# Attention beside a state-space layer on one core: a weight band by two heads, single tail matmuls, another load layout, C swapped by DMA, and a new order of all steps

## The chip, the core and the metric

The kernel runs on one core of one Trainium2 chip. The core has five engines, each with a queue of its own that is worked off strictly in order: TensorE (PE: matmuls and transposes; its weight loads are shown as PEld), VectorE (DVE), ScalarE (ACT), GpSimd (POOL) and SyncE (SP, which here only issues transfers). Transfers run on 16 DMA engines. Matmul results stand in eight PSUM banks and have to be evicted by DVE or ACT. The metric is the device time of one execution in microseconds (us).

## The reference

Two independent layers on inputs of 2048 tokens by 448 features (bf16), their outputs beside each other.

```python
# A: 16 heads of 28; each token attends to 8 tokens, at distances 0, 2, ..., 14
q, k, v = split(x @ wqkv)
idx = pos[:, None] - arange(8) * 2
logits = where(idx >= 0, einsum("bhsd,bhswd->bhsw", q, k[idx]) * 28 ** -0.5, -1e9)
a = einsum("bhsw,bhswd->bhsd", softmax(logits), v[idx]).reshape(B, S, D) @ wo

# B: diagonal complex state space of 448 states
Lam_bar = exp(dt * Lam)
Bu = einsum("bld,pd->blp", x, ((Lam_bar - 1) / Lam)[:, None] * (B_re + 1j * B_im))
h[t] = Lam_bar * h[t - 1] + Bu[t]
b = 2 * einsum("blp,dp->bld", h, C_re + 1j * C_im).real + x * Dskip
out = concatenate([a, b], axis=-1)
```

## The kernel before

**The order.** The kernel has no loops over its work. A string, `ORDER`, lists 580 steps; the last loop of the function calls them one by one, and each step issues one or a few instructions to the queue of an engine. `QK021@24` is step `QK` with arguments 0, 2, 1, and 2 and 4 are the PSUM banks that it takes. A full stop or an equals sign at the end puts an eviction on ACT or DVE. As the queues work in order, `ORDER` alone sets what each engine does next; semaphores hold an instruction until its data have come. The first loads (x, wqkv, B) stand ahead of the string and are issued first. A transfer also waits until the one eight before it is done.

**Part A, attention.** x is loaded in natural layout (`xnA`, row `t * 128 + p` on partition p) and transposed: the first 1024 tokens by PE against an identity (`XI`, `XA`, `XH`, evicted by `xi`, `xa`, `xh`), the others by DMA. The feature dimension of 448 is three blocks of 128 and a tail of 64; two tails, of two token blocks, stand in the two halves of the partitions, so that two 64-row matmuls run beside each other. `QK` and `QS` make q and k (evicted by `qk`, `qh`), `V_` makes v (`v`). For logits, `P` multiplies q on DVE by k shifted by four distances at a time (128x2048 elements, L379), into one of seven buffers, and `E_` sums over each head's features by matmuls against a 0/1 matrix of 32 columns, four of them beside each other in tiles of 128x32 (L391, and L395 for the last heads). `lt` scales the logits to SBUF, `TD` transposes them by DMA (L413), `sma`, `smb` and `smc` are the softmax (maximum and sum on DVE, exponential on ACT).

The weighted sum over v is a matmul against a band matrix, with tokens on both axes. `AL` shifts the weights by matmuls, `al` evicts them to a buffer `Ak` with room between them, `ad` writes that to memory (L497), and `sp` reads it back skewed by one position a row (L503), which gives the band `PT` (128 partitions, 12 blocks, 16 / HS groups, HS * 135 elements). HS = 4 heads are interleaved in a row: neighbouring positions of one head stand four elements apart. `AV` (L528, L534) has v as the stationary operand (32 columns, four heads beside each other) and the band as the moving one, with a step of HS. `W_` (L547) multiplies by wo, `w` evicts to `ya`, `ow` stores.

**Part B, state space.** Tokens are taken in groups of T = 4; the state's 448 complex values are G = 7 groups of 64 real and 64 imaginary ones. `xt` (L696) and `BD` (L672) transpose x and B by DMA to `xTB` and `BT`. `BU` multiplies them (helper `part`, L244, which also serves `QK` and `V_`), `BR` (L723) and `UP` add rotated earlier tokens in the same bank, `z` and `y` evict to `Z` and `Z3`. On DVE `sa` rotates by a table (`ty`, `tf`, `ts` make it), `sb` scans over 256 positions (L764) and `sd` rotates back; `DN`, `dn` and `H_`, `h` carry the scanned state to the other tokens. For the two inner tokens that is done without PE: `sw` swaps real and imaginary halves by DMA, `hp` multiplies by a column (28 steps, all on ACT: L834, L836), `hy` and `hz` add on DVE (L840, L845). C is loaded (`LC`), reordered (`ci`) and transposed by DMA (`CD`) to `Cw`; `ca` multiplies the swapped halves by a column on ACT (two instructions of 64 partitions a group, L684), `cs` multiplies by the other column and adds on DVE (L688). `C` (L859) sums over seven groups, `c` adds x times Dskip (`xd`, L849) on DVE (L867 to L870), `oc` stores. The last tile is done in two halves (`CH`, L884; `ch`, L894; `oh`).

**Order around the change.** PE's queue runs: transposes; q, k and v with the `E_` steps between; from `BU000` on part B with `AL` between; eight `AV`; some `W_` with rotations and corrections; eight `AV`; `W_`, `H_` and the first `C`; and at the end ten `C` and two `CH` steps almost alone. DVE does the 28 `P` steps almost without a break, the first softmax's `sma0` among them, then softmaxes, evictions, scans and corrections, at the end the additions of `c`. SP issues the loads, then `xt0`, `xt1`, `TD0`, `xt2`, `xt3`, `BD`, C's loads and Dskip (`LC`, `LD`), `TD1`, `CD`, wo, and the band's transfers.

Of the kernel before, what the change touches and what calls it, by code (L numbers as in the profile page):

```python
# [15 lines left out]
HALO = 14  # L16
# [4 lines left out]
G = 7  # L21
HS = 4
# [22 lines left out]
z10. BU401@74 BU400 ad0 pm0 smb1 BR11 z11= ts03 smc1 BU010@12 AL1@0 BR21 BU011 al1. BU111@53 xd2 ad1 z40. ca3 cs3 z21.
BU110 BR41 BR12 z12. BR02 z02= BU310@07 BR13 sp0 z13= z41. ts13 BU410@65 xd0 pm1 BR03 z03= sp1 ts04 ca6 ca1 cs6 UP1
BU211@41 BU311 BU411 BR32 z32= BR42 z42= BU210 BR22 ca2 AX@0 BR33 xd1 y1. z33= UP0 y0. BR43 sa0 ax. pm4 cs1 z43= AL2@6
al2. ad2 BU600@32 AL3@0 z22. ts23 al3. ad3 BU601 z60. BU511@64 BR23 z23. cs2 sb0 BU510 sd0 ca4 BR52 z52. UP3 UP4 y4=
UP2 BR61 z61. AV020@0 y3. av020. AV000@3 av000. AV001@6 adx y2= cs4 sa2 sb2 AV011@2 av011= sd2 av001. pm2 AV030@7
AV010@0 AV031@5 AV021@3 av030. BU611@16 ts14 ca5 BU610 BR62 av010. av031. DN0@7 z62. DN1@0 dn1 dn0 sp2 BR53 z53.  # L50
W_20@5 UP5 W_10@1 av021. BR63 W_01@2 W_30@3 y5. ts24 sa4 DN3@4 dn3 DN2@0 sb4 ca0 w20. cs0 z63. ab hp021 hp020 cs5
W_11@7 W_00@5 w01. w11. UP6 spx y6. sp3 AV101@4 av101. AV110@2 w10. w00= AV100@7 AV131@6 AV130@4 av110. AV121@1 sw0
hp120 hp121 AV111@2 AV120@5 av131. dn2 ow11 W_31@0 av111. av100. av120. sd4 DN4@6 sa6 DN5@2 av121. dn4 hp010 ow01 ow20
# [10 lines left out]
def kernel(  # L64
# [45 lines left out]
    def ps(dt=F32):  # L110
        return ps_p.tile([128, 512 if dt == F32 else 1024], dt, tag=f"ps{banks.pop(0)}", name="ps")
# [866 lines left out]
```

## Time and profile before

| | us |
|---|---|
| runs (3) | 128.70, 129.04, 129.21 |
| median | 129.04 |
| profiled execution, first to last instruction (span) | 127.4 |

The page is of one profiled execution, whose time lies within its span and what lies around it: the median of the runs is 1.6 us above the span. PE is busy for 120.3 us of it, DVE 116.0, ACT 104.4, POOL 21.6; PE's clock is granted in full (0.999). The DMA engines move 22.33 MB in 49156 packets.

How to read it: a PE duration contains the pipeline's latency, so that a matmul of 448 columns shows 352 ns while 70 of them pass in 13.36 us (191 ns each); PE's pace is read from starts. In the groups, the columns are line, engine, operation, output<-input, shapes, count, then busy us, mean ns of one, and the idle time ahead of them with what ended it. In stages, each engine has its busy us and a count. In the chain and the time line the columns are start, length, what. SPq is the queue of SP: issues, not the transfers.

### The profile page before, as it was taken

The numbers are of one execution on the slowest core, as the hardware profiler recorded it, in microseconds if no ns is written. First come the engines' busy times: TensorE is split into PE (matmuls) and PEld (weight loads), VectorE is DVE, ScalarE is ACT, GpSimd is POOL, SyncE is SP. The second block draws the span as 40 slices with busy tenths as digits, with TensorE's granted clock in tenths as the row PEclk, the third lists the DMA queues.
The fourth block names the chain that finished last, engine by engine and source line by source line (L and its number), as shares of the span: only waits on it lengthen the run. The fifth ranks groups of instructions, "written<-read, shape, count | busy, mean of one in ns | idle before, by whom it ended". The sixth has DMA issues, their size and how long they took to land.

```text
span 127.4 us, 2887 instructions
## 1 busy us (share of the span) xinstructions
PE 120.3 (94%) x1044; PEld 61.5 (48%) x1053; DVE 116.0 (91%) x223; ACT 104.4 (82%) x205; POOL 21.6 (17%) x41
## 2 busy tenths in 40 slices
PE   6979999999999998999999999999999999999990
PEld 6532443433344442344443558556865545545560
DVE  5679899999998999999899999999999999999651
ACT  0859999997898997899999999999999999961000
POOL 6801000000000000200599992000000000000000
PEclk9999999999999999999999999999999999999999
DMA  3897999899999999487879999993254431234742
GB/s 99 239 223 161 311 263 158 157 231 217 162 246 181 204 217 222 127 165 146 249 320 192 180 339 244 161 132 84 91 145 114 123 109 36 75 110 133 228 144 72
DMA packets 49156, 22.33 MB, mean 175 GB/s; under 512 B 35735, under 2 KB 48599, under 8 KB 49143
## 3 DMA queue, kind: packets, MB, share of 16 engines
q1 hardware_dynamic: 48936, 22.12, 75.7%
q8 instruction: 8, 0.13, 0.4%
q10 hardware_dynamic: 207, 0.04, 0.2%
q14 instruction: 5, 0.04, 0.1%
HBM read 9.86 MB, written 6.37 MB: 127 GB/s over the span
## 4 chain that ended last, share of the span: by engine, by line
PE 82%; DMA 8%; SPq 5%; issue 2%; DVE 0%
PE ps L244 36%; PE ps L859 16%; PE ps L547 10%; PE ps L534 6%; DMA BT<-Bn 5%; PE ps L723 4%; DMA wq<-in_A_wqkv_dram 3%; PE ps L391 2%; SPq L696 2%; SPq L128 2%; PE ps L789 1%; PE ps L348 1%; PE ps L884 1%; PE ps L395 1%; PE ps L461 1%
## 5 line engine op out<-in xcount | busy, mean ns | idle before, releaser
L379 DVE TENSOR_TENSOR pr<-qf,kf 128x2048 bf16<-128x2048 bf16 x24 | 28.2, 1236 | 0.0
L244 PE MATMUL ps<-xbuf,BT 128*128 128x512 bf16 (+1 forms) x107 | 23.5, 380 | 0.9 <-DMA BT<-Bn 0.4
L859 PE MATMUL ps<-Cw,Z 128*128 128x448 bf16 x105 | 20.6, 352 | 0.0
L244 PE MATMUL ps<-xT,wq 128*128 128x512 bf16 (+1 forms) x93 | 19.5, 379 | 0.6 <-issue 0.5
L859 PEld LDWEIGHTS <-Z 128*128 128x128 bf16 x105 | 10.3, 98 | 9.7 <-issue 0.2
L244 PEld LDWEIGHTS <-BT 128*128 128x128 bf16 (+1 forms) x112 | 8.7, 97 | 12.2 <-issue 2.7
L547 PE MATMUL ps<-wo,oT 128*128 128x448 bf16 x64 | 13.9, 353 | 0.0
L244 PEld LDWEIGHTS <-wq 128*128 128x128 bf16 (+1 forms) x96 | 7.7, 97 | 11.2 <-issue 2.3
L114 ACT CAST Z<-ps 128x512 bf16<-128x512 f32 (+1 forms) x24 | 11.7, 522 | 1.3 <-issue 0.9
L935 POOL MEMSET PT<- 128x4320 f32 x3 | 11.0, 3703 | 8.9 <-DVE Z L114 8.9
L244 PE MATMUL ps<-wq,xT 128*128 128x448 bf16 (+1 forms) x64 | 11.7, 353 | 0.0
L684 ACT ACTIVATE ctmp<-Cw,c2t 64x448 f32<-64x448 bf16 x14 | 9.3, 666 | 0.2
L547 PEld LDWEIGHTS <-oT 128*128 128x128 bf16 x64 | 6.2, 98 | 5.5 <-issue 0.2
L534 PE MATMUL ps<-PT,v_s 128*32 128x135 bf16 (+1 forms) x256 | 8.6, 299 | 0.3 <-issue 0.3
L114 ACT CAST ya<-ps 128x448 bf16<-128x448 f32 (+1 forms) x15 | 7.7, 554 | 1.3 <-DMA out_dram<-ya 1.2
L114 ACT CAST oT<-ps 128x512 bf16<-128x512 f32 x15 | 8.3, 613 | 0.1
L244 PEld LDWEIGHTS <-xT 128*128 128x128 bf16 (+1 forms) x64 | 5.2, 97 | 6.0 <-issue 1.5
L114 ACT CAST v_s<-ps 128x448 bf16<-128x448 f32 x16 | 7.8, 545 | 0.1
L114 ACT CAST qf<-ps 128x512 bf16<-128x512 f32 x12 | 6.9, 593 | 1.0 <-PE ps L349 0.7
L534 PEld LDWEIGHTS <-v_s 128*32 128x32 bf16 x256 | 7.1, 111 | 0.8 <-issue 0.5
L723 PE MATMUL ps<-Z,R 128*128 128x512 bf16 x21 | 7.1, 379 | 0.0
L911 POOL MEMSET Z<- 128x14 bf16 x1 | 0.1, 110 | 38.0 <-ACT v_s L114 38.0
(170 smaller groups left out, 221.5 us busy)
## 6 DMA issues: line engine op xcount, KB each, us to landing
PT<-pd SPq DMA_DIRECT2D x16, 156.0 KB, 4.4
out_dram<-ya SPq DMA_DIRECT2D x16, 112.0 KB, 1.8
out_dram<-xbuf SPq DMA_DIRECT2D x15, 112.0 KB, 1.8
pd<-Ak SPq DMA_DIRECT2D x2, 640.0 KB, 3.6
xbuf<-in_A_x_dram SPq DMA_DIRECT2D x2, 448.0 KB
xnB<-in_B_x_dram SPq DMA_DIRECT2D x4, 224.0 KB, 6.3
xnB<-in_B_x_dram SPq DMA_DIRECT2D x4, 192.0 KB, 5.6
PT<-Z SPq DMA_DIRECT2D x6, 128.0 KB, 2.4
```

The source lines that it names most:

```text
L114: (ACT.copy if e == "A" else V.tensor_copy)(o, i)
L128: SP.dma_start(wq[:, 0:3, c + d:c + d + n], wq_r[:, :, c + d:c + d + n])
L244: PE.matmul(o, l, r, start=(first and i == 0), stop=(not first and i == len(pairs) - 1 and not more[s]))
L379: V.tensor_tensor(t[:], q.unsqueeze(1).to_broadcast((128, 4, 512)), k4, ALU.mult)
L391: PE.matmul(acc[s][32 * i:32 * i + 32], E[:, f, ws, :], t[:, i, :], start=(f == 0 and ws == 0), stop=False)
L534: PE.matmul(p[32 * hh:32 * hh + 32, 128 * bl:128 * bl + n], v_s[:, t, 4 * hg + hh, :], PT[:, t % NS, (4 * hg + hh) // HS, (4 * hg + hh) % ...
L547: PE.matmul(p[:, 0:D], late["oT"][:, b // 4, hg, par, 128 * (b % 4):128 * (b % 4) + 128], late["wo"][:, hg, :], start=(hg == 0), stop=(hg ...
L684: ACT.activation(t[a:a + 64, 0:D], Cw[b:b + 64, g, :], ACTF.Copy, scale=c2t[a:a + 64, g:g + 1])
L696: SP.dma_start(xTB[:, :, :, 128 * cb:128 * cb + 128].rearrange("p a b c -> p (a b) c"), xnB[:, cb].rearrange("p j d -> p (j d)"), transpos ...
L723: PE.matmul(pp["z", g, j][:], rot(g, 0), late["Z"][:, g, j - 1, :], start=False, stop=True)
L859: PE.matmul(p[:, 0:D], z, Cw[:, g, :], start=(g == 0), stop=(g == G - 1))
L935: POOL.memset(late["PT"][:, 4 * i:4 * i + 4].rearrange("p t g n -> p (t g n)").bitcast(F32), 0.0)
```

## The change

- `HS` is 2: two heads interleaved in the band. `AV` steps by two elements, `sp` copies twice as many pieces of half the length.
- The tail matmuls of 64 rows are steps of their own (`QT`, `VT`, `BH`); the main ones are by half (`QS`, `VM`, `BU` take one bank and issue three matmuls). `part`, `two`, `QK` and `V_` go.
- x of the first 1024 tokens is loaded with four consecutive rows on a partition (`LX`), one contiguous piece for each partition; the evictions `xi`, `xa`, `xh` write with a step of four to put the tokens in order.
- All loads are steps of the order (`LX`, `LQ`, `LH`, `LV`, `LY`, `LB`, `LN`, `TX`, `WX`).
- C: `CS` writes `Cw` with its halves swapped to a buffer by two transfers, `ca` and `cb` multiply the two by their columns in place (seven each, on ACT or DVE as the order says: of `ca` one on ACT, of `cb` three), `cs` adds two groups at a time on DVE.
- `hp` can go to DVE: 15 of 28 do.
- Buffers that rotated are named by slot in the order (`P`, `ty`, `smc`, `w`, `c`).
- All steps stand in a new order. In SP's queue the loads of C and Dskip stand ahead of the transposes `xt` and `BD`, half of B's load between them, the order of transposes is `xt1`, `xt3`, `xt2`, `BD`, `xt0`, and `TD0` follows. `sma0` stands behind the last `P` on DVE, one `rb` ahead of the first. Evictions of `z` and `y` are on ACT, but for two `y`.

The diff, cut to its core:

```diff
-HS = 4
+HS = 2
...
-    prp = pool("a_pr", bufs=7, c=cl)
+    prp = pool("a_pr", c=cl)
...
+    def LX(a, b):
+        k = a // 4
+        SP.dma_start(xnA[:, a:b], A_x[0, 512 * k:512 * k + 512].rearrange("(p t) d -> p t d", t=4)[:, a - 4 * k:b - 4 * k])
...
     def xi(h, k, e):
-        p, c = pp["xi", h], 256 * h
+        p = pp["xi", h]
...
-            evict(e, xT[:, 0, 0:2, c:c + 256], p[:, 0:512].rearrange("p (f n) -> p f n", f=2))
+            evict(e, xT[:, 0, 0:2].rearrange("p f (n t) -> p f t n", t=4)[:, :, 2 * h:2 * h + 2],
+                  p[:, 0:512].rearrange("p (f t n) -> p f t n", f=2, t=2))
...
-    def QK(u, m, k):
-        p = two("qk", u, m)
-        part(("qk", u, m), k,
...
+    def QS(u, m, s):
+        p = pp["qk", u, m, s] = ps()
         for kt in range(3):
-            PE.matmul(p[:], wqk(m, slice(0, 128), kt), xT[:, 0, 4 * s + kt], start=(kt == 0), stop=False)
-        PE.matmul(p[:], wqk(m, slice(64 * s, 64 * s + 64), 3), xT[64 * s:64 * s + 64, 0, 3], start=False, stop=True)
+            PE.matmul(p[:], wqk(m, slice(0, 128), kt), xT[:, u, 4 * s + kt], start=(kt == 0), stop=False)
+
+    @op
+    def QT(u, m, s):
+        r = slice(64 * s, 64 * s + 64)
+        PE.matmul(pp["qk", u, m, s][:], wqk(m, r, 3), xT[r, u, 3], start=False, stop=True)
...
-    def ca(g):
-
-        t = pp["ctmp", g] = smp.tile([128, 512], F32, tag="z", name="ctmp", bufs=2)
+    def CS():
         for a, b in ((0, 64), (64, 0)):
-            ACT.activation(t[a:a + 64, 0:D], Cw[b:b + 64, g, :], ACTF.Copy, scale=c2t[a:a + 64, g:g + 1])
+            SP.dma_start(late["oT"][a:a + 64, 0].rearrange("p a b n -> p (a b n)")[:, 0:G * D],
+                         Cw[b:b + 64].rearrange("p g n -> p (g n)"))
+
+    def scaled(e, t, c):
+        if e == "A":
+            ACT.activation(t, t, ACTF.Copy, scale=c)
+        else:
+            V.tensor_scalar(t, t, c, None, ALU.mult)
+
+    @op
+    def ca(g, e):
+
+        scaled(e, swc(g), c2t[:, g:g + 1])
+
+    @op
+    def cb(g, e):
+        scaled(e, Cw[:, g, :], c1t[:, g:g + 1])
 
     @op
     def cs(g):
-        V.scalar_tensor_tensor(Cw[:, g, :], Cw[:, g, :], c1t[:, g:g + 1], pp["ctmp", g][:, 0:D], ALU.mult, ALU.add)
-
+        n = 2 if g < 6 else 1
+        o = Cw[:, g:g + n, :].rearrange("p g n -> p (g n)")
+        V.tensor_tensor(o, o, swc(g, n), ALU.add)
...
-    def BU(g, jp, k):
...
+    def BU(g, j):
+        p = pp["z", g, j] = ps()
+        for f in range(3):
+            PE.matmul(p[:], BT[:, g, f, :], xTB[:, j // 2, 4 * (j % 2) + f, :], start=(f == 0), stop=False)
+
+    @op
+    def BH(g, j):
+        r = slice(64 * (j % 2), 64 * (j % 2) + 64)
+        PE.matmul(pp["z", g, j][:], BT[r, g, 3, :], xTB[r, j // 2, 3, :], start=False, stop=(j == 0))
...
-    def hp(k, j, g):
+    def hp(k, j, g, e="A"):
...
-            ACT.activation(t, late["SW"][:, NC * g:NC * (g + 1)], ACTF.Copy, scale=bcol[:, j - 1, g:g + 1])
+            i, c = late["SW"][:, NC * g:NC * (g + 1)], bcol[:, j - 1, g:g + 1]
...
+        if e == "A":
+            ACT.activation(t, i, ACTF.Copy, scale=c)
+        else:
+            V.tensor_scalar(t, i, c, None, ALU.mult)
```

Of the new order, first the loads, then the stretch from the last `E_` steps to the first of part B, and the band's copies:

```
LX02 LX24 LQ00 LQ11 LQ01 LX48 LQ10 LH13 LH01 LV LB110 LH03 LQ21 LH10 LY1 LY2 LH02 LY0 LQ20 LH12 WX LN10 LB001 LD
WU@0 LN00 LB100 XI0@0 TX3 TX0 TX2 TX1 PP@1 LB021 LB111 xi00= LB011 LB120 LC pcopy xi01. pa XI1@2 xi10= LB010 xi11.
XI2@3 LB121 QS000@1 xi20. pb pd_ QS030@3 LB101 QS010@2 QT000 XH1@0 XA10@4 xt1 LB000 pc XA11@5 LB020 LN11 LN01 xt3
xt2 pe ty0@0 ty5@1 BD xt0 QS020@6 tf0 tf5 xa10= pf pg xa11. QS031@4 xh1. ts00 qk000. QS021@5 rb0 QS001@0 VM100@1
QT010 qk010= P000@0 QT001 ts05 ts10 ts20 QT020 QT031 QT030 QT021 qk001. qk021. qk031. qk030. VM000@7 P001@1 qk020.
P021@2 P020@3 VM111@2 VM101@5 QS051@4 ts15 ty2@0 tf2 ts25 QS050@6 QS011@3 QT011 QT050 VT111 ty1@1 qk011. P010@4
...
qk141. qk150. E_06 lt00 qk120. P121@4 QS160@7 QS140@3 qk131. QS121@4 QS161@0 QT160 QT121 lt01 QT140 qk140. QT161
...
VM500@7 VT410 VT511 hc1 VT400 VT011 P131@3 P151@4 P150@5 P130@1 v011. VT500 VT401 v401. v511. ts16 v400. E_13 E_15
P141@2 E_14 ts26 BU21@0 BU00@1 ty3@1 v500. BU30@3 BU11@7 BU10@5 P161@1 P160@2 E_16 BH10 BH11 BH00 v410. sma0 smb0
OZ z10. lt11 lt10 TD1 OP CS tf4 ab dk BH21 BH30 z30. z00. BU12@2 BR11 BU20@5 BU01@4 z11. pm3 BU13@3 smc0@0 BH12 xd0
BH01 pm1 BH20 BH13 BR01 BR12 z12. AL1@7 al1. z01. AL0@1 BU50@2 BU40@7 BU03@4 pm4 al0. ad1 pm0 pm2 sma1 tf3 z20. wo
ad0 rb3 smb1 ts03 smc1@0 ca0= cb2= ca3= cb0= BU31@5 BU41@1 BU02@6 BH02 BH41 BH40 z40. BH03 BH50 BH31 BR13 z13. BR02
...
BR52 z52. BR43 z43. DN0@6 dn0 BR61 z61. BU62@7 UP4 y4. BR53 z53. AV001@5 av001. AV010@2 av010. AV031@4 av031.
AV011@6 ad3 sp2 spx AV020@1 AV021@5 AV030@0 AV000@2 sp3 cs4 av011. UP5 BU63@4 BH63 BH62 sd2 DN2@6 BR62 y5. sa4
```

More of the change, by code (lines that the diff above doesn't have):

```diff
@@ L48 @@
[L48 to L52, printed above, removed]
@@ L234 @@
     Cr = s1.tile([128, 4, 2, D], BF16, tag="Cr")
+    prt = prp.tile([128, 7, 4, 512], BF16, tag="pr", name="pr")
+    ltb = prp.tile([128, 2, 512], BF16, tag="lt", name="lt")
     pp = {}
     ops = {}
[L238 to L251 removed]
     def op(f):
@@ L912, in OZ @@
         late["sc"] = s5
-        late["m"] = 0
     @op
@@ L924, in OP @@
                       late["ya"].rearrange("p k n -> p (k n)")[:, 0:2560]]
-        late["n"] = 0
     @op
```

204 lines of the change are left out of this document (91 added, 113 removed).

## Prediction

> **What bounds the kernel now.** I read the page's head first, then the busy time by stage, then the chain that ended last, then single stretches of the time line.
>
> ```profile
> span 127.4 us, 2887 instructions
> PE 120.3 (94%) x1044; PEld 61.5 (48%) x1053; DVE 116.0 (91%) x223; ACT 104.4 (82%) x205; POOL 21.6 (17%) x41
> ```
>
> Three engines are nearly full, so the mean shares decide nothing. The stages do (columns: length of the stage, then busy time of PE, PEld, DVE, ACT, POOL with counts, clock, DMA share, GB/s):
>
> ```profile
> 3.60:9.53 5.93, 5.06 (x43) 2.89 (x44) 4.32 (x20) 3.96 (x14) 2.46 (x9) 1.00 0.96 224
> 9.53:49.24 39.71, 38.56 (x276) 15.69 (x281) 38.61 (x60) 37.26 (x78) 0.61 (x1) 1.00 1.04 207
> 49.24:114.10 64.86, 64.10 (x645) 35.08 (x651) 63.05 (x125) 61.48 (x114) 16.05 (x11) 1.00 0.66 160
> 114.10:124.60 10.50, 10.03 (x60) 5.54 (x57) 7.86 (x20) 0.97 (x2) 0.00 (x0) 1.00 0.52 168
> ```
>
> Up to 49.24 us PE, DVE and the DMA engines are all full (DMA share 1.04). From there to 114.10 PE and DVE are both full: PE idles 0.76 us, DVE 1.81. So a gain on one of them alone gives nothing; the later of the two sets the end. Only the last 10.5 us belong to PE alone. The chain and DVE's time line show the three points at which they meet:
>
> ```profile
> 24.43 1.41 PE ps L391 x24
> ...
> 42.46 6.74 DMA BT<-Bn
> ...
> 109.43 13.36 PE ps L859 x70
> 122.79 1.35 PE ps L884 x14
> ...
> 124.17 0.39 DVE xbuf L894
> ```
>
> ```profile
> 48.27 2.36 DVE L379 TENSOR_TENSOR pr<-qh_t,kh 128x2048 bf16<-128x2048 bf16 x2
> ...
> 113.41 0.69 DVE L845 TENSOR_TENSOR Z<-Z,PT 128x1024 bf16<-128x1024 bf16 x1
> ```
>
> ```profile
> 49.24 2.22 PE L244 MATMUL ps<-xbuf,BT 128*128 128x512 bf16 x11 [0.43 <-DMA BT<-Bn]
> ```
>
> First point: the state part's first matmul (BU) starts at 49.24, when the transposed weights BT land. Second: DVE ends its last product for the logits (P) at 50.63. Third: DVE ends the last scan correction (hz) at 114.10, and PE needs it in the C step that it has just begun; from there PE runs to 124.14 without a gap, 10.04 us. An output addition of 0.39 and the last store follow, to 127.4.
>
> **The change, part by part.**
>
> *Weight band by two heads.* The matmuls that apply the attention weights (AV) read every fourth element of the band, in the change every second. Their rate now:
>
> ```profile
> 76.89 4.11 PE L534 MATMUL ps<-PT,v_s 128*32 128x135 bf16 x128
> 80.93 0.39 PE L244 MATMUL ps<-xbuf,BT 64*128 64x512 bf16 x2
> ```
>
> From 76.89 to 80.93 128 matmuls pass, four beside each other: 32 sets in 4.04 us, 126 ns for a set of some 133 columns, 0.95 ns a column. The logits' matmuls (L391, the same 128x32 tiles, operand contiguous) pass six sets of 512 columns in 1.41 us, a change of tile shape included: 0.46 ns a column. So AV runs at half the rate, and its step is the difference that I see. If a step of two gives the full rate, a set takes some 60 ns: 64 sets by 66 ns, 4.2 us off PE. If it doesn't, 0. No row has a step of two. I take 4.2: steps of one and four give 0.46 and 0.95, so if the time goes with the bytes spanned, a step of two gives 0.95 / 2 = 0.48, about the contiguous rate. [...]
>
> The band's copy out of memory (sp) gets pieces of 156 bytes for 312, with the same bytes.
>
> ```profile
> PT<-pd SPq DMA_DIRECT2D x16, 156.0 KB, 4.4
> ```
>
> ```profile
> 80.80 2.13 SPq L503 DMA_DIRECT2D PT<-pd  x4
> ```
>
> ```profile
> 88.54 0.66 PE L534 MATMUL ps<-PT,v_s 128*32 128x135 bf16 x16
> ```
>
> If a piece costs the same whatever its size, landing goes from 4.4 to 8.8 us. The cover is the work between the first eight AV steps and the second eight: sp3 overwrites what the first eight read, in both versions. That stretch takes 7.5 us of PE before (81.0 to 88.5); by the new order it has eight W steps and some rotations, of about the same length. The four issues (2.13) and 4.4 leave 1 us of margin, so the cost is 0 to 3.4 us; I take 0, as the bytes don't grow.
>
> *Matmul tails as own steps.* The number of matmuls of every shape stays. By the two orders PE changes tile shape 45 times for 48. At some 0.1 us (1.41 less six sets at 0.22) that is 0.3 us off PE.
>
> *Swapped C by DMA, and scalings moved.* I counted DVE's instructions from its last P to its last hz, 122 before and 132 after, and priced them by these rows:
>
> ```profile
> L834 ACT ACTIVATE PT<-PT,bcol 128x512 bf16<-128x512 bf16 x8 | 5.8, 745 | 0.0
> L684 ACT ACTIVATE ctmp<-Cw,c2t 64x448 f32<-64x448 bf16 x14 | 9.3, 666 | 0.2
> L688 DVE SCALAR_TENSOR_TENSOR Cw<-Cw,c1t,ctmp 128x448 bf16<-128x448 bf16 x7 | 4.6, 675 | 0.0
> L114 DVE CAST Z<-ps 128x512 bf16<-128x512 f32 x5 | 3.4, 687 | 0.2 <-PE ps L723 0.2
> L114 DVE CAST Z<-ps 128x256 bf16<-128x256 f32 x6 | 2.4, 418 | 0.0
> L114 DVE CAST oT<-ps 128x512 bf16<-128x512 f32 x2 | 1.3, 674 | 0.0
> L114 DVE CAST ya<-ps 128x448 bf16<-128x448 f32 x2 | 1.2, 617 | 0.0
> L666 DVE TENSOR_TENSOR R<-Is,co 128x896 bf16<-128x896 bf16 x2 | 2.2, 1084 | 0.0
> L849 DVE TENSOR_TENSOR xnB<-xnB,dsk 128x1792 bf16<-128x1792 bf16 x4 | 4.3, 1083 | 0.0
> L869 DVE TENSOR_TENSOR xbuf<-ps,xnB 128x384 bf16<-128x384 f32 x8 | 4.4, 549 | 0.2 <-PE ps L859 0.2
> L867 DVE TENSOR_TENSOR xbuf<-ps,xnB 128x448 bf16<-128x448 f32 x7 | 4.1, 618 | 2.0 <-PE ps L859 2.0
> L845 DVE TENSOR_TENSOR Z<-Z,PT 128x1024 bf16<-128x1024 bf16 x4 | 2.6, 686 | 0.0
> L757 DVE TENSOR_TENSOR vv<-Z,tab 128x512 bf16<-128x512 bf16 x3 | 1.3, 426 | 0.1
> L649 DVE TENSOR_SCALAR kM<-iot,fT 128x256 f32<-128x256 f32 x7 | 2.4, 346 | 0.0
> L705 DVE COPY dsk<-dsk 128x384 bf16<-128x384 bf16 x1 | 0.3, 254 | 0.0
> ```
>
> ```profile
> 40.41:42.70 2.29, 1.96 (x7) 1.00 1.13 209
> ```
>
> Out of this stretch go: seven L688 (4.73), five wide and four narrow Z evictions to ACT (3.44 and 1.67), one oT and one ya eviction (1.29), one R (1.08, now before the first P), one Dskip product (1.08, now after), two L869 less one L867 (0.48): 13.8 us. In come: the first softmax's maximum (five instructions; the window row has them and the ends of two neighbours, 1.96), four sums of C (448 or two times 448 columns, 0.4 and 0.6 by L757 and L845: 2.2), and 25 multiplications by a column, ten of C and 15 of the correction. The last kind isn't in the trace on bf16. Its floor is the copy L705, 254 at 384 columns (270 to 290 here); its ceiling L757, 426. I take 340, as L649 is the same operation: 8.5 us, 7 to 10.5. In all 12.7 come in: DVE's stretch gets shorter by 1.1, and as much of the shown durations overlaps with the next instruction (two products of L379 in 2.36 us) and ten more instructions overlap more, I take 1.8 (bounds 0 and 3.5). ACT loses 14 L684 and 15 products at 745, 20 us, and takes some 8 back (the evictions as priced above, four scalings of C at 0.65): it is off the path, and its earlier evictions let DVE and PE wait less. Of DVE's 1.81 us of idle time I take 0.8 as gone (0 to 1.8).
>
> C's swap is two transfers more, 0.8 MB, while the DMA share is 0.66; DVE reads them late, behind both softmax ends, so 0.
>
> *First loads and all steps reordered.* Before the first P DVE gets one R (1.08) more and the first softmax's maximum (1.9) less; three evictions of x, 2048 columns, now write every fourth element, 0 to 1.0 us (twice the 0.5 ns a column between L757 and L845). The last P stays at 50.6, by 0.5 either way. PE's 0.87 us of idle time between 3.60 and 9.53 may go, but PE waits for P at E steps before 49, so it gives nothing.
>
> The DMA order changes more. SP now issues C's loads and Dskip before the last transposes, and the first softmax's transpose (TD) behind them:
>
> ```profile
> 37.27 1.26 SPq L413 DMA_TRANSPOSE attn<-lt  x1
> ...
> 47.36 0.57 SPq L268 DMA_DIRECT2D Cr<-in_B_C_re_dram  x1
> ...
> 49.72 0.58 SPq L701 DMA_DIRECT2D dsk<-in_B_Dskip_dram  x1
> ```
>
> ```profile
> 40.00:50.00 10.00, 9.37 (x83) 4.06 (x83) 9.66 (x13) 9.91 (x20) 0.11 (x1) 1.00 1.10 212
> ```
>
> The five issues from 47.36 to 50.30 (2.8 us) go ahead of what the first BU needs, TD's 1.26 goes behind: 1.5 us later by issue. By bytes (0.9 MB at 212 GB/s less TD's 0.26 MB) it is 3.1. Pauses of SP ahead of its transposes, such as this one, may go in the new order:
>
> ```profile
> SPq L413 <- ACT kh L114: 1.1, 1, 1.1
> ```
>
> The contiguous x loads may save some of it too; I don't price that. So BU starts between 48.8 (49.24 less PE's wait of 0.43) and 51.5; I take 50.0, near the middle, and TD's landing, 1.26 more issue and its flight, at 51.5. DVE, done with P at 50.6, then waits 0.9 us for it: a new wait. Behind it in DVE's queue stands all that this engine does to the end.
>
> **The sum.** DVE: 51.5 + 63.5 - 1.8 - 0.8 = 112.4 for the last hz (before 114.10). PE needs that one for the fifth of seven matmuls of a C step, six C steps and 1.35 us follow: 10.2, so 122.6. PE by itself: 50.0 + 74.9 (49.24 to 124.14) - 4.2 - 0.3 = 120.4, earlier, so DVE decides. DVE's own additions behind hz, 24 instructions for 19, take about 10, the same end. 122.6 for 124.14 is 1.5 us less. Against the profiled execution (span 127.4) it gives 125.9; the median of the runs is 129.04, 1.6 above the span, and I take 129.04 - 1.5 = **127.5 us**.
>
> **Rivals.**
>
> *PE at its own floor.* If the multiplications cost their floor and idle time goes, hz ends at 110 and PE's 120.4 decides: 3.7 less, 125.3. For it: ACT is relieved. Against it: DVE's time line has no slack that the change frees for certain.
>
> *AV stays at half rate* (also the case in which the change doesn't do what it says): PE needs 50.0 + 74.9 - 0.3 = 124.6, past DVE: 129.5, from 128.3 (BU at 48.8) to 131. For it: no row shows a step of two. [...]
>
> *Slower: the transposes land late.* Place: SP's queue between C's loads and TD. With the price by bytes and no pause saved, BU starts at 51.5 and TD lands at 53.5 or later; DVE idles 3 us and hz ends at 114.4 or later. From a landing of TD at 53.0 the gain is gone; at 54.5 the time is 130.5. For it: the DMA share is over 1 in this very stage. Against: C's pieces of 896 bytes move faster than a transpose's.
>
> **Chances.** Forecast (126.3 to 128.4) 0.46, PE's floor 0.14, AV unchanged 0.17, late transposes 0.18, others (a late band, friction of banks at the end) 0.05, mostly slower. About 0.5% is what a measurement here can tell from none: 128.4 and 129.7. Faster 0.59, same 0.13, slower 0.28. The range is 125.0 to 130.4: it leaves out the ends of floor and late transposes.
>
> **What would show it.** AV: a set near 60 ns right, near 126 wrong. BU's first matmul near 50 and a DVE wait for the DMA behind the last P. DVE's multiplications near 340 ns. The last hz near 112.4, with PE running from there to the end in about 10.2 us. If PE idles over 2 us behind 50, or AV waits for the band, I am wrong.

## The result, and the profile after

The changed kernel takes 137.1 us (median of 5 runs, 135.07 to 139.39) beside 129.04 before: a ratio of 1.0515 with an interval of 1.0428 to 1.0602. Runs more than 1.5% above the fastest of their kernel are left out of a ratio, so the ratios below, and not the medians, are compared; 1.0515 of 129.04 is 6.6 us slower. The forecast was 127.5. The profiled execution took 135.97 us.

The head of the page after the change:

```profile
span 134.3 us, 2882 instructions
PE 122.4 (91%) x1044; PEld 58.8 (44%) x1053; DVE 121.4 (90%) x235; ACT 93.8 (70%) x190; POOL 22.6 (17%) x41
...
PEclk9999999999999999999999996799999999999998
```

PE is busy 2 us longer although the number of matmuls is the same, DVE 5 us longer, ACT 11 us less, and the granted clock has a dent at 60% of the span. The stages (length, then busy PE, PEld, DVE, ACT, POOL with counts, clock, DMA share, GB/s), cut where PE's long waits at the start are over (16.26), where the state part's first matmul (BU) starts, at the last matmul ahead of a wait (79.03), where the half rate behind that wait ends (85.41), and shortly ahead of the first C step (104.70):

```profile
3.60:16.26 12.66, 9.02 (x47) 4.75 (x49) 8.62 (x27) 8.60 (x19) 2.47 (x9) 1.00 0.97 240
16.26:53.96 37.70, 37.31 (x272) 14.93 (x275) 36.79 (x52) 33.96 (x71) 1.77 (x4) 1.00 1.10 198
53.96:79.03 25.07, 24.77 (x194) 11.01 (x193) 24.27 (x44) 23.76 (x48) 15.96 (x9) 1.00 0.88 199
79.03:85.41 6.38, 3.74 (x11) 1.18 (x9) 5.61 (x15) 2.17 (x5) 0.00 (x0) 0.73 1.27 224
85.41:104.70 19.29, 19.18 (x366) 11.37 (x368) 17.90 (x42) 18.38 (x39) 0.00 (x0) 1.00 0.87 130
104.70:130.96 26.26, 25.80 (x140) 13.28 (x138) 25.64 (x59) 6.18 (x12) 0.00 (x0) 1.00 0.35 111
```

Two stages are new. Up to the point from which PE runs on without long waits, 12.66 us go by with 9.02 of PE, where before it was 5.93 with 5.06; BU, at 49.24 before, now starts at 53.96. And from 79.03 to 85.41 PE is busy for 3.74 of 6.38 us at a mean clock of 0.73. From 85.41 to the end PE has no gap to speak of, as before.

DVE's time line, its start before (first fence), and its start and some later rows after (second; start, length, engine, line, operation):

```profile
4.82 0.62 DVE L114 COPY xT<-ps 128x512 bf16<-128x512 bf16 x2 [0.56 <-PE ps L288]
9.20 0.69 DVE L114 COPY xT<-ps 128x1024 bf16<-128x1024 bf16 x1 [0.48 <-PE ps L305]
9.81 2.76 DVE L379 TENSOR_TENSOR pr<-qf,kf 128x2048 bf16<-128x2048 bf16 x2
```

```profile
4.57 1.30 DVE L125 COPY xT<-ps 128x512 bf16<-128x512 bf16 x1 [0.31 <-PE ps L296]
...
13.78 2.43 DVE L125 COPY xT<-ps 128x1024 bf16<-128x1024 bf16 x1 [2.78 <-PE ps L318]
...
20.44 4.63 DVE L386 TENSOR_TENSOR pr<-qf,kf 128x2048 bf16<-128x2048 bf16 x4
...
53.06 2.36 DVE L386 TENSOR_TENSOR pr<-qh_t,kh 128x2048 bf16<-128x2048 bf16 x2 [0.20 <-PE ps L398]
...
58.04 0.25 DVE L728 COPY dsk<-dsk 128x384 bf16<-128x384 bf16 x1
58.20 0.90 DVE L729 COPY dsk<-dsk 128x64 bf16<-128x64 bf16 x1
...
60.33 0.95 DVE L441 RECIPROCAL zc<-zc 128x128 f32<-128x128 f32 x1
...
65.11 0.86 DVE L654 TENSOR_SCALAR kM<-iot,fT 128x256 f32<-128x256 f32 x1
...
70.98 2.39 DVE L697 TENSOR_SCALAR oT<-oT,c2t 128x448 bf16<-128x448 bf16 x1
73.30 0.32 DVE L697 TENSOR_SCALAR Cw<-Cw,c1t 128x448 bf16<-128x448 bf16 x1
...
118.87 1.89 DVE L873 TENSOR_TENSOR Z<-Z,PT 128x1024 bf16<-128x1024 bf16 x3
```

Three things are to be seen. A copy of 512 columns, two of which took 0.62 us, takes 1.30 now that it writes every fourth element, and one of 1024 columns 2.43 for 0.69. The first product for the logits (P) starts at 20.44 instead of 9.81; the new order has moved some of this by itself (e1 below, without the strided copies, has 14.39), but the last P also ends later, at 55.34 (the instruction behind it starts then) for 50.63. And three instructions in the middle are many times too long: the copy of 64 columns lasts 0.90, longer than the one of 384 ahead of it (0.25); L654 lasts 0.86 for 0.35 elsewhere; a multiplication by a column lasts 2.39 where the next one, of the same shape, lasts 0.32. Beside these three stand GpSimd's memsets:

```profile
58.21 0.86 POOL L957 MEMSET wo<- 128x896 f32 x1 [2.35 <-issue]
59.90 3.71 POOL L959 MEMSET PT<- 128x4320 f32 x1 [0.83 <-DMA Cw<-Cn]
...
64.66 1.17 POOL L955 MEMSET ya<- 128x1280 f32 x1
65.76 7.48 POOL L959 MEMSET PT<- 128x4320 f32 x2
```

The first long one ends as the memset of 58.21 does (59.10, 59.07). The second starts inside the memset of 64.66 and ends near that one's end (65.97, 65.83). The third ends as the pair from 65.76 does (73.37, 73.24). All three are copies or multiplications by a column, with one tensor operand, from SBUF to SBUF; I call these one-operand below. Not everything with one operand is late: the reciprocal at 60.33 takes 0.95 us inside the memset of 59.90, as it does in the kernel before where no memset runs (53.05), and an eviction out of PSUM takes its usual 0.42 there (68.56) beside the memsets of 61.87. PE at the two places, the start and behind the scan:

```profile
8.96 2.29 PE L351 MATMUL ps<-xT,wq 128*128 128x512 bf16 x5 [0.45 <-ACT xT L125]
...
13.80 0.81 PE L351 MATMUL ps<-xT,wq 128*128 128x512 bf16 x3
...
81.94 0.40 PE L800 MATMUL ps<-Z,R 128*128 128x256 bf16 x1 [2.64 <-DVE Z L795]
82.13 1.48 PE L735 MATMUL ps<-xbuf,BT 128*128 128x512 bf16 x3
...
86.93 0.81 PE L735 MATMUL ps<-xbuf,BT 128*128 128x512 bf16 x3
88.00 2.19 PE L539 MATMUL ps<-PT,v_s 128*32 128x135 bf16 x128
```

At 8.96 five matmuls of 512 columns take 2.29 us, the half rate; from 13.80 on three take 0.81. (The clock column gives 1.00 for this stage, so that the half rate is read from the pace. In e5 PE is busy for the same 1.00, 1.00 and 0.64 us of 9 to 10, 10 to 11 and 11 to 12, with as many matmuls, and there the column gives 0.50.) Ahead of 81.94 PE waits 2.64 us for DVE's scan (L795), and then runs at half rate again: three matmuls in 1.48 at 82.13, 0.81 at 86.93. The clock's row for that moment:

```profile
82.00:83.00 1.00, 1.00 (x4) 0.38 (x5) 1.00 (x4) 0.00 (x0) 0.00 (x0) 0.50 1.23 307
```

The last row of PE's time line is the good part: 128 matmuls with the attention weights (AV) in 2.19 us, half of before's 4.11.

### The profile page after: what moved, and what is told of

Same layout as the page of the kernel before. It is cut to its first block, busy times and chain, and to the rows that moved or that the text cites. A ratio compares the mean times of both kernels' runs of the same rounds, so it can differ in the third digit from the quotient of the medians.

```text
span 134.3 us, 2882 instructions
## 1 busy us (share of the span) xinstructions
PE 122.4 (91%) x1044; PEld 58.8 (44%) x1053; DVE 121.4 (90%) x235; ACT 93.8 (70%) x190; POOL 22.6 (17%) x41
## 4 chain that ended last, share of the span: by engine, by line
PE 49%; DVE 17%; ACT 12%; DMA 10%; POOL 3%; issue 3%; SPq 2%; POOLq 1%; DVEq 0%; ACTq 0%
PE ps L351 14%; PE ps L887 12%; PE ps L515 5%; ACT oT L125 4%; DVE xT L125 4%; PE ps L356 3%; DMA PT<-Z 3%; DVE oT L697 3%; DMA out_dram<-ya 3%; POOL PT L959 3%; PE ps L398 2%; PE ps L552 2%; DMA Cw<-Cn 2%; DMA wo<-in_A_wo_dram 2%; ACT Z L125 2%
## 5 line engine op out<-in xcount | busy, mean ns | idle before, releaser
L351 PE MATMUL ps<-xT,wq 128*128 128x512 bf16 x80 | 21.0, 403 | 3.3 <-DVE co L621 1.7
L735 PE MATMUL ps<-xbuf,BT 128*128 128x512 bf16 x80 | 21.7, 397 | 0.2
L125 ACT CAST Z<-ps 128x512 bf16<-128x512 f32 (+1 forms) x33 | 15.6, 527 | 5.9 <-PE ps L747 5.5
L351 PEld LDWEIGHTS <-wq 128*128 128x128 bf16 x84 | 8.2, 102 | 14.8 <-issue 7.1
L735 PEld LDWEIGHTS <-BT 128*128 128x128 bf16 x84 | 8.0, 101 | 9.8 <-issue 2.5
L515 PE MATMUL ps<-wq,xT 128*128 128x448 bf16 x48 | 10.4, 353 | 0.2 <-ACT qh_t L125 0.2
L125 ACT COPY xT<-ps 128x256 bf16<-128x256 bf16 (+2 forms) x5 | 5.2, 1087 | 4.0 <-PE ps L318 2.0
L125 DVE COPY xT<-ps 128x512 bf16<-128x512 bf16 (+1 forms) x3 | 4.9, 1672 | 3.1 <-PE ps L318 2.8
L515 PEld LDWEIGHTS <-xT 128*128 128x128 bf16 x48 | 4.4, 98 | 6.0 <-issue 2.4
L125 ACT CAST kf<-ps 128x512 bf16<-128x512 f32 x11 | 6.1, 597 | 0.7 <-PE ps L356 0.7
```

Source lines behind the costliest of these rows:

```text
L125: (ACT.copy if e == "A" else V.tensor_copy)(o, i)
L351: PE.matmul(p[:], wqk(m, slice(0, 128), kt), xT[:, u, 4 * s + kt], start=(kt == 0), stop=False)
L515: PE.matmul(p[:, 0:D], xT[:, b0 // 4, 4 * s + kt, c + par:c + 256:2], wq[:, kt, 2 * D:3 * D], start=(kt == 0), stop=False)
L735: PE.matmul(p[:], BT[:, g, f, :], xTB[:, j // 2, 4 * (j % 2) + f, :], start=(f == 0), stop=False)
```

## The experiments

After the result I had three theories. **A, the start**: partition-major loads force strided evictions, and these delay the first P and everything behind it. **B, GpSimd's memsets**: in the new order they stand beside one-operand DVE instructions, which wait for them; this makes the scan late. **C, the clock**: it is PE's half rate, at the start and behind the wait at 79, that costs. The prediction's own rival, **late transposes**, and the disputed point **who sets the end**, PE or DVE, were tested with them. Differences in us are ratio differences times 129, and a ± is the intervals of the two runs taken together. The diffs are cut to their core, and of a line of the order only the part that moves is shown. e1 to e6, e9, e10 and e12 start from the changed kernel; e7, e8 and e11 from the kernel before.

**e1_contig.** The first x loads and their evictions as before, all else as changed.

```diff
-        SP.dma_start(xnA[:, a:b], A_x[0, 512 * k:512 * k + 512].rearrange("(p t) d -> p t d", t=4)[:, a - 4 * k:b - 4 * k])
+        SP.dma_start(xnA[:, a:b], xA_r[:, a:b])
...
-        evict(e, o.rearrange("p (n t) -> p t n", t=4), i.rearrange("p (t n) -> p t n", t=4))
+        evict(e, o, i)
...
```

> The changed kernel with its first loads of x and their evictions as before (contiguous), all else kept. Theory A (the early evictions that write every fourth element cost the start): the DVE eviction of 1024 columns falls from 2.43 us to about 0.7, those of 512 from 1.3 to about 0.65, TensorE's waits of 1.37 and 2.03 us behind 5.7 and 14.2 us shrink to under 0.7 each, the first state matmul moves from 53.96 to 50 to 51 us, and the time falls by 3 to 4 us, to about 132. Rival (the order of the first steps holds the start): the evictions get shorter but the first logits product stays behind 18 us, and the time falls by under 1.5 us. Rival (late transposes): the start gets earlier, VectorE then waits over 2 us for the first softmax transpose, and the time falls by under 1.5 us.

Measured: 1.042 (1.0345 to 1.0495), 1.2 ± 1.5 us better than the change, so by its time alone not to be told from none; e6 beside e5 tries the same edit again. DVE's and PE's time lines:

```profile
9.59 0.68 DVE L125 COPY xT<-ps 128x1024 bf16<-128x1024 bf16 x1
...
14.39 4.63 DVE L384 TENSOR_TENSOR pr<-qf,kf 128x2048 bf16<-128x2048 bf16 x4
```

```profile
26.79 4.06 PE L349 MATMUL ps<-xT,wq 128*128 128x512 bf16 x17 [1.76 <-DMA xT<-xbuf]
...
51.22 3.40 PE L733 MATMUL ps<-xbuf,BT 128*128 128x512 bf16 x14 [0.94 <-DMA xbuf<-xnB]
...
79.99 0.28 PE L798 MATMUL ps<-Z,R 128*128 128x256 bf16 x1 [3.29 <-DVE Z L793]
```

The evictions are back at 0.68, the first P at 14.39, the last P's end at 51.67 (3.7 earlier), and BU at 51.22 (2.7 earlier). Theory A holds for the start, but at most a part arrives at the end: PE now waits for transposes by DMA (1.76 and 0.94), which the slow start had hidden, and longer for the scan (3.29 for 2.64).

**e2_chop.** GpSimd's six memsets cut into 30 short ones, to let DVE in between (the expectation counts five and 22).

```diff
...
-            POOL.memset(late["PT"][:, 4 * i:4 * i + 4].rearrange("p t g n -> p (t g n)").bitcast(F32), 0.0)
+            for q in range(8):
+                w = H // HS // 2
+                POOL.memset(late["PT"][:, 4 * i + q // 2, w * (q % 2):w * (q % 2) + w].rearrange("p g n -> p (g n)").bitcast(F32), 0.0)
```

> The changed kernel with GpSimd's five memsets cut into 22 shorter ones, same bytes. Theory B (a copy or a multiplication by a column on VectorE waits for the end of GpSimd's running memset): the three long VectorE instructions, 0.90, 0.86 and 2.39 us, fall to at most 0.7 each (0.2 to 0.35 by themselves plus what is left of a short memset), VectorE gains 2.3 to 3 us, TensorE's wait of 2.9 us at 79.0 falls to under 1 us and its half rate from 82 to 85 us goes; the time falls by 3 to 4.5 us. Rival (the multiplication waits for the DMA that swaps C, or is slow on its first use): the 2.39 us stays and the time falls by under 1 us.

Measured: 1.0841 (1.0772 to 1.091), 4.2 ± 1.4 us worse. DVE, and GpSimd beside it:

```profile
65.35 9.25 DVE L654 TENSOR_SCALAR kM<-iot,fT 128x256 f32<-128x256 f32 x1
```

```profile
66.56 7.89 POOL L963 MEMSET PT<- 128x540 f32 x16
```

One instruction of 0.35 us lasts 9.25, to the end of sixteen memsets in a row (74.45). So the place of theory B is right and the form I gave it is wrong: shorter memsets don't make the wait shorter. Here it lasted to the end of the whole row.

**e3_warm.** Matmuls on a constant tile, overwritten at once, ahead of three early steps and of the scan's rotation, to keep PE's clock up.

```diff
+        for _ in range({(0, 0): 12, (3, 0): 6, (2, 0): 8}.get((m, s), 0) if u == 0 else 0):
+            PE.matmul(p[:, 0:128], wz[:], wz[:], start=True, stop=True)
...
```

> The changed kernel with matmuls on zeros, whose result is overwritten, in TensorE's waits: 26 ahead of the first query and key projections, 46 ahead of the scan's second matmul. Theory C (TensorE runs at half rate behind a wait, and this costs by itself): the pitch of 512 columns falls from 427 to 215 ns between 7 and 12 us and between 82 and 85 us; the time falls by 1.5 to 3.5 us. Rival (the waits cost, the rate only fills time in which TensorE would wait anyway): the pitch falls and the time moves by under 0.7 us.

Measured: 1.0484 (1.0388 to 1.058), 0.4 ± 1.7 us better. The half rate is gone (six matmuls of 512 columns at 9.30 take 1.46 us, and the clock is 1.0 from 79 to 86), the first P comes at 18.43, the last one ends at 53.51 for 55.34, and BU, at 53.04, now waits 0.92 us for the transposes. The time can't be told from the change's; a gain of up to some 2 us isn't excluded. So theory C is shown for the start's delay, and not for the end.

**e4_band4.** The changed kernel with the band by four heads again.

```diff
-HS = 2
+HS = 4
```

> The changed kernel with the weight band by four heads again, all else kept. If TensorE sets the end of the changed kernel, a set of four weight matmuls goes back from about 66 to 126 ns and the time rises by 3.5 to 4.5 us, to about 140. Rival (VectorE sets the end, as the prediction had it): the sets get longer and the time rises by under 1.5 us. Rival (the pieces of 156 bytes cost): the band lands earlier and the time falls.

Measured: 138.95 to 144.28, median 142.4; the runs lie too far apart for an interval. Its profiled execution has two things at once, AV's slower rate on PE and this on DVE:

```profile
64.97 9.33 DVE L654 TENSOR_SCALAR kM<-iot,fT 128x256 f32<-128x256 f32 x1
```

AV is back at 4.07 for 2.19. But L654, untouched by this edit, lasts 9.33 us, to the end of the memsets (74.30, 74.15), where in the change's profiled execution it slipped in after 0.86. So the edit's effect is mixed with the memsets', and e12 was made to part them.

**e5_twoin.** The remedy that follows from e2: the nine one-operand DVE instructions that fall beside the memsets or close to them written in two-operand forms (a product with a column broadcast, a maximum of a tile with itself), in the same places (the expectation calls them eight).

```diff
...
         else:
             V.tensor_scalar(t, t, c, None, ALU.mult)
+        elif e == "T":
+            V.tensor_tensor(t, t, c.to_broadcast((128, D)), ALU.mult)
...
-        V.tensor_copy(dsk[:, 512:896], dsk[:, 0:384])
+        V.tensor_tensor(dsk[:, 512:896], dsk[:, 0:384], dsk[:, 0:384], ALU.max)
```

> The changed kernel with the eight VectorE instructions that stand beside GpSimd's memsets written with two tensor operands (the phase of two frequencies, the two copies of Dskip, five scalings of C), same place, same values. Theory B, sharpened by the last runs (a one-operand copy or multiplication on VectorE waits while GpSimd runs memsets back to back, and is let in only at some joints; the two-operand forms run beside them): no VectorE instruction between 56 and 75 us is longer than 1.3 us, VectorE gains 2.5 us or more, TensorE's wait near 79 us and its half rate behind it shrink, the time is 131 to 133 us and the runs spread by under 1.5 us where they spread by 4. Rival (the long ones wait for data, or the spread comes from the clock): one of them stays above 2 us, or the time stays above 134 us.

Measured: 1.027 (1.0186 to 1.0354), 3.2 ± 1.6 us better than the change.

```profile
65.08 0.48 DVE L657 SCALAR_TENSOR_TENSOR kM<-iot,fT,mag 128x256 f32<-128x256 f32 x1
...
70.58 0.62 DVE L702 TENSOR_TENSOR oT<-oT,c2t 128x448 bf16<-128x448 bf16 x1
```

Nothing waits: the same two steps last 0.48 and 0.62 beside the same memsets. (The form has a price of its own, 0.62 us for the 0.33 that the multiplication takes away from memsets.) PE's wait near 79 falls to 1.67 us and no half rate follows it (the clock is 1.00 from 70 to 90). Theory B is shown: the form of the instruction decides whether DVE waits.

**e6_contig_twoin.** e1 and e5 together (both diffs above).

> The last edit together with contiguous first loads and evictions of x. If the two losses are separate, the gains add: 128.5 to 130.5 us, the kernel before reached again. If the late transposes of the new DMA order take the start's gain back (the first state matmul waits for the transposes at 50 to 51 us, the softmax for its own), it stays at 130.5 to 132 us.

Measured: 1.0139 (1.0076 to 1.0202), 4.9 ± 1.4 us better than the change, about the sum of both (1.2 and 3.2), and 1.7 ± 1.4 better than e5, which is e1's edit again. No version of the new order measured faster, and it is still behind the kernel before. PE and DVE:

```profile
51.92 3.40 PE L740 MATMUL ps<-xbuf,BT 128*128 128x512 bf16 x14 [2.10 <-DMA xbuf<-xnB]
...
78.72 0.28 PE L805 MATMUL ps<-Z,R 128*128 128x256 bf16 x1 [1.64 <-DVE Z L800]
```

```profile
48.85 2.36 DVE L386 TENSOR_TENSOR pr<-qh_t,kh 128x2048 bf16<-128x2048 bf16 x2 [0.19 <-PE ps L398]
53.21 0.29 DVE L422 TENSOR_TENSOR attn<-attn,mk 128x256 bf16<-128x256 bf16 x1 [1.99 <-DMA attn<-lt]
...
114.12 1.90 DVE L878 TENSOR_TENSOR Z<-Z,PT 128x1024 bf16<-128x1024 bf16 x3
```

With both faults mended the prediction's rival is in plain sight: DVE is done with P at 51.2 and waits 1.99 us for the softmax's transpose (TD); PE waits 2.10 for BU's. The last scan correction (hz) ends at 116.0, before 114.10.

**e7_before_band2.** The kernel before with the band by two heads, alone.

```diff
-HS = 4
+HS = 2
```

> The kernel before with the weight band by two heads and nothing else. The sets of four weight matmuls take about 66 ns for 126, 4.2 us less on TensorE. If VectorE and TensorE were both full (the reading of the prediction), VectorE's last correction near 114 us holds the end and the time falls by under 1 us, to 128.2 to 129.2. Rival (TensorE alone set the end): the time falls by 3 to 4.5 us, to about 125.

Measured: 1.0159 (1.0101 to 1.0217), slower by 2.0 us, as neither side expected. PE, and SP's queue:

```profile
91.28 0.31 PE L534 MATMUL ps<-PT,v_s 128*32 128x135 bf16 x8 [2.39 <-DMA PT<-pd]
...
94.94 0.30 PE L534 MATMUL ps<-PT,v_s 128*32 128x135 bf16 x8 [1.40 <-issue]
```

```profile
83.38 3.61 SPq L503 DMA_DIRECT2D PT<-pd  x4
```

Four issues of the band's copies take 3.61 us (before 2.13), the sixteen 14.0 in all (before 7.8), and AV's second half waits 2.39 us for them. For the 1.40 us further on, at a place where the kernel before waits 0.29, the trace names no releaser. In the old order the smaller pieces take back what the faster AV gives, and 2 us more; the edit touches only the band.

**e8_before_pm.** The kernel before with partition-major first loads and strided evictions (e1's diff the other way round).

> The kernel before with the first x loads partition-major and the evictions that write every fourth element, and nothing else. Theory A: the evictions take about twice as long, the first logits product moves from 9.8 to 11.5 us or later, and as VectorE and TensorE are full behind it the time rises by 1.5 to 3 us. Rival (the larger rows make the loads land earlier, the evictions have room): the time moves by under 0.7 us.

Measured: 1.0106 (1.0015 to 1.0198): 1.4 us slower. DVE's time line:

```profile
9.87 2.42 DVE L114 COPY xT<-ps 128x1024 bf16<-128x1024 bf16 x1
```

The same 2.42 for 1024 columns, the first P 2.3 us later (12.09) and the last one 1.6 later. So the layout of the loads costs by itself in the old order too, 0.2 to 2.6 us by the interval.

**e9_scanfirst.** e1, with DVE's instructions ahead of the scan reordered: the steps tf4, tf3 and dk ahead of the softmax, most scalings of C behind the scan, and the three left before it in two-operand form.

```diff
-BH10 BH11 BH00 v410. sma0 smb0
+BH10 BH11 BH00 v410. tf4 tf3 dk sma0 smb0
...
-BR32 BR22 z22. sd0 cb4= cs2 cs6 AL3@2
+BR32 BR22 z22. sd0 ca3= cb1= ca1= cs0 ca6= ca2= cb4= cs2 cs6 AL3@2
```

> Contiguous first loads as in the first of these runs, and VectorE's order changed: the phases of two frequencies and the copies of Dskip ahead of the first softmax (beside no memset), the first scan ahead of most scalings of C, three early scalings with two tensor operands. If the wait near 77 us comes from the scalings that stand ahead of the scan in VectorE's queue, TensorE's 1.8 us there go to under 0.5, with no half rate; the waits for the transposes (1.0 and 2.1 us at 25 and 50 us in the last kernel with contiguous loads) stay. Time 129 to 130.5 us against 131.4 for that kernel. Rival (VectorE is late for another reason, the sum of its work): the wait only moves and the time stays at 131 us or more.

Measured: 1.0199 (1.0148 to 1.0249), no better than e6. PE's wait for the scan is gone, the time is not: its profiled execution has others instead, of 2.26 us for weights at 20.90 and of 1.33 for an eviction on ACT. That execution took 133.53 us and the other three 131.37 to 131.76, so these waits need not be theirs. A missed expectation.

**e10_late_c.** e9, with C's loads issued behind TD (its reordering and its transposes move back with them) and the transposes of x for attention ahead of three loads, to get the transposes landed earlier.

```diff
-qh101. VM010@1 TD0 CD0 qk121.
+qh101. VM010@1 TD0 LC qk121.
...
-WU@0 LN00 LB100 XI0@0 TX3 TX0 TX2 TX1 PP@1
+WU@0 XI0@0 TX3 TX0 TX2 TX1 LD LN00 LB100 PP@1
```

> The same, with the loads of C issued behind the first softmax's transpose instead of ahead of the state part's transposes, and part of the loads for the state part behind the transposes of x. If the new DMA order makes the transposes late (the rival of the prediction), the first state matmul starts by 50 us, TensorE's waits at 25 and 50 us fall from 3.1 to under 1 us together, and the time falls by 1.5 to 2.5 us more, to 126.5 to 128.5, under the kernel before. Rival (the DMA engines are full there in any order): the waits stay or move to the softmax or to the band, and the time stays at 129 to 130.5 us.

Measured: 134.81 to 137.44 us, the fastest 3.4 above e9's fastest (131.37). PE and DVE, in an execution of 137.19:

```profile
51.70 3.40 PE L735 MATMUL ps<-xbuf,BT 128*128 128x512 bf16 x14 [2.52 <-ACT v_s L125]
```

```profile
57.66 1.29 DVE L125 COPY Cn<-Cr 128x896 bf16<-128x896 bf16 x4 [2.83 <-DMA Cr<-in_B_C_im_dram]
...
73.47 2.53 DVE L697 TENSOR_SCALAR oT<-oT,c2t 128x448 bf16<-128x448 bf16 x1
```

BU starts hardly earlier than in e6 (51.70 for 51.92), now behind an eviction on ACT; DVE waits 2.83 for C; the memsets move back and hold up one more multiplication, 2.53. This DMA order only moved the wait; that none would do better is not shown.

**e11_before_band2_pool.** e7 with four of the last eight band copies issued from GpSimd's queue.

```diff
-            SP.dma_start(late["PT"][32 * s:32 * s + 32, sl:sl + 4, :, 32 * HS * s:32 * HS * s + 39 * HS].rearrange("p t g n -> p (t g) n"),
+            (POOL if g > 1 and s % 2 else SP).dma_start(late["PT"][32 * s:32 * s + 32, sl:sl + 4, :, 32 * HS * s:32 * HS * s + 39 * HS].rearrange("p t g n -> p (t g) n"),
```

> The kernel before with the band by two heads (131.4 us by itself), and four of the last eight copies of the band issued from GpSimd's queue, which is idle there, instead of SP's. If the 156-byte pieces cost by SP's issue time (14.0 us for sixteen copies against 7.8), the two waits of TensorE inside the weight matmuls (2.4 and 1.4 us) fall to under 1 us together and the time falls by 2 to 3 us, to 128.5 to 129.5; by VectorE's reading it is not below 128. Rival (the pieces cost in the DMA engines, 19.0 us for 15.3): the waits stay and the time stays within 0.7 us of 131.4.

Measured: 1.0137 (1.0094 to 1.018), for e7's 1.0159. PE's waits of 2.39 and 1.40 become one:

```profile
90.66 0.31 PE L534 MATMUL ps<-PT,v_s 128*32 128x135 bf16 x8 [1.65 <-DMA PT<-pd]
```

Less waiting, but the copies take 6.2 us to land from that queue (SP's 4.9), and the intervals overlap: 0.3 ± 0.9 us. How much of e7's cost is issue and how much the transfer of small pieces stays open.

**e12_repaired_band4.** e6 with the band by four heads, so that AV's step is tried without the memsets' noise.

```diff
-HS = 2
+HS = 4
```

> The changed kernel with contiguous first loads and the eight two-operand forms (131.4 us), with the weight band by four heads again. If TensorE sets the end of the repaired kernel, the step of two is worth what it was in the changed one (3.5 to 4.2 us): the time is 134.5 to 136. [...]

Measured: 1.0389 (1.0333 to 1.0444), 3.2 ± 1.1 us slower than e6. PE and DVE:

```profile
82.75 4.09 PE L539 MATMUL ps<-PT,v_s 128*32 128x135 bf16 x128
```

```profile
117.17 1.89 DVE L878 TENSOR_TENSOR Z<-Z,PT 128x1024 bf16<-128x1024 bf16 x3
```

In this order three quarters of AV's gain arrive at the end, so PE's work there is on the path; it isn't DVE alone that decides the end. The last hz itself ends 3.0 us later than in e6 (119.1 for 116.0), and from the first softmax to it DVE idles 4.9 us for 1.6: DVE waits for what PE brings later.

## Why the prediction was wrong

The sum itself closes, which shows which terms failed. I had the last hz at 112.4 and the span at 125.9. Measured: 120.8 (118.87 and 1.89) and 134.3, each 8.4 later. Of these, 3.8 are the start of DVE's stretch (55.34 for 51.5), and 4.5 its length (65.4 for 60.9); the part behind hz is 13.5 in both.

*First loads: failed, the costliest step of the start.* I took "0 to 1.0 us" for three strided evictions and held the last P at "50.6, by 0.5 either way". The price came from a floor between two other DVE rows, neither of them strided; the three take 5.0 us (1.30, 1.28, 2.43) for 1.5 in e1 (0.43, 0.42, 0.68), and ACT's copies slow down as well (0.72 for 0.37 at 256 columns). My list counted DVE's evictions and left out that PE needs each before its next projections. I also wrote off PE's early idle time as of no effect; the idle time grew, PE stayed at half rate to 13.5 us, and the last P ended 4.7 us late. e1 gives 3.7 us of that back at the last P, e8 shows the same evictions on the kernel before. At the end of the kernel that is worth 1.7 ± 1.4 us (e6 beside e5), where the transposes are late too.

*DVE's stretch: the price was right, a resource was missing.* The multiplications by a column were to take 340 ns; alone they take 0.32 to 0.35. But three one-operand instructions waited for GpSimd: 0.90 for 0.18, 0.86 for 0.35, 2.39 for 0.33, together 3.3 of the 4.5 us. I had counted DVE's instructions with their durations and never laid GpSimd's memsets beside them; 8.5 us of the new work is of the kind that waits. Why they wait no run shows; e5, where two-operand forms beside the same memsets took 0.48 and 0.62, shows that the form decides it. Idle time adds 2.0: I left DVE 1.0 us of it, and by the windows it idles 3.0 from 53.96 to 104.70 (0.80, 0.77, 1.39). The rest of its work takes some 0.8 less than I priced, which closes the 4.5.

*Weight band: the rate right, the path half right.* A set was to take some 60 ns; 32 sets take 2.19 us, 68 each, for 126. Counted from start to start over all 64 sets, PE gains 4.3 us where I took 4.2. But I booked the gain on PE, whose sum was "earlier, so DVE decides"; e12 shows 3.2 us of it at the end, so PE's work in that stage was on the path. The step that failed here is to add up DVE and PE apart and take the later one: in between DVE waits for PE.

*The band's copies: right in the new order, for a reason that isn't general.* I took 0 with bounds 0 to 3.4. After the change the last landing on record is at 95.8 and the second half of AV starts at 98.6 without a wait, so they are hidden; in the old order 2.4 us of waits are theirs, and 1.4 more stand beside them (e7). The price per piece, that "the bytes don't grow", was wrong: issuing sixteen copies takes 14.0 us for 7.8.

*Late transposes: the rival was real, hidden in the result.* TD landed at 54.0 for my 51.5, past the rival's threshold of 53.0. In the change no one waits for it, as the last P is later still. In e6, where P is back at 51.2, DVE waits 1.99 us for it, and its stretch then takes 62.8. That closes e6's sum too: 53.2 for 51.5 and 62.8 for 60.9 make 3.6 us, and its span is 129.5 for the 125.9 forecast.

*Sum and ranges.* The chance of 0.28 for slower rested on the transposes and little else. The range's upper end, 130.4, lacked two mechanisms which together make 4.9 us (e6): strided evictions, which I had bounded by rows that don't write with a stride, and the memsets, which I hadn't bounded at all. One of my signs of being wrong came true, PE idle for over 2 us behind 50 (2.64 at 79), but for a reason that I hadn't named. *Tails* (0.3 us) were not measured apart.

PE's half rate behind the wait at 79 belongs to the second: three matmuls take 1.48 for 0.81 until 85.4, some 1.7 us, and no such stretch follows e5's wait of 1.67. e3, which removed the half rate and left what PE waits for, shows no gain that can be told from none, with up to some 2 us not excluded; so I count it as a consequence, which is argued and not shown.

What stays open: why e9, which removed the scan wait of 1.64 us, gained nothing; how e7's cost divides, and what its wait of 1.40 us is for; and whether an order exists in which transposes and C's loads both come in time.

## What to carry to other kernels

Before one-operand copies and multiplications in SBUF are moved on DVE, lay GpSimd's time line beside DVE's: here one of 0.35 us waited for a whole row of memsets (9.25 in e2), and writing it with two operands removed the wait (0.48 in e5). Price a strided write by a strided row, and if there is none, let the range hold what was measured here, three to 3.6 times the contiguous duration (1.30 us for 0.43, 2.43 for 0.68), with all who wait for it. A change that makes one engine's read faster by smaller DMA pieces has to be summed with the queue that issues them (14.0 us for 7.8 in e7), in the order in which it will run.

## What the runs showed of the hardware

- A one-operand copy or multiplication on DVE isn't reliably let in between back-to-back memsets: with sixteen short ones it waited to the end of them all (9.25 us in e2). The same instruction beside the same long memsets got in early in three executions (0.47 in e3, 0.86 in the change, 1.42 in e1) and not in another (9.33, e4), which fits with the change's runs spreading over 4.3 us and e5's over 1.9. Reciprocals (0.95) and evictions out of PSUM (0.42) didn't wait.
- TensorE fell to half rate behind a wait of 2.64 us and stayed there for 3.3 us; in e9 half rate followed a wait of 2.26 (twelve matmuls of 512 columns in 4.45 us). Waits of 1.67 (e5), 2.10 (e6) and 2.52 (e10) left it alone (fourteen in 3.40 us behind each of the last two), but at e5's start the clock column falls to 0.50 at 8.1 us, behind no wait of more than 1.57, so the length of the last wait alone doesn't decide it.
- A copy with every fourth bf16 element written takes 1.30 us for 512 columns on DVE (0.42 contiguous in e1), 2.43 for 1024 (0.69).
- By the trace's DMA records (e7 and before), the band's pieces of 156 bytes take 18.6 ns of a DMA engine each (21.0 in the change), those of 312 bytes 29.9: the cost is between one per piece and one per byte. In the profile before, pieces of 896 bytes (C's and Dskip's, 49.5 to 52.5 us) take 47.1 ns, those of the transposes of 256 bytes (46 to 49 us) 21.8: 19.0 and 11.7 bytes a ns.
